# A fused linear-attention and gated feed-forward kernel: five hand-written emission orders replaced

## Chip, cores and metric

The kernel runs on one core of one Trainium2 chip. The metric is the device time of one execution in microseconds. Three executions of the kernel before gave 298.26, 298.84 and 298.95 us; the median, 298.84 us, is the time before.

## What is computed

The inputs are q, k and v of shape 8 x 8 x 576 x 64 (batch, heads, sequence, head size) and three weights: gate and value of 512 x 1536, output of 1536 x 512. First a linear attention, then a gated feed-forward block on its result:

```python
q_s = softmax(q, axis=-1)                      # over the 64 of a head
k_s = softmax(k, axis=2)                       # over the sequence
kv  = einsum('bhsd,bhse->bhde', k_s, v)
x   = einsum('bhsd,bhde->bhse', q_s, kv)       # then 4608 tokens x 512
g   = x @ w_gate
out = (g * sigmoid(g) * (x @ w_val)) @ w_out   # 4608 x 512, float32
```

## The kernel before

**Stages.** The 4608 tokens are worked through in chunks. Batch 0 of the attention is done in a prologue that the change leaves as it is. After it stand nine chunks, each with its own order of work: chunk -1 (tokens 0 to 575, order `PLAN_B`), chunk 0 (tokens 576 to 1023, `PLAN_0`), chunks 1 to 5 (512 tokens each, `PLAN`), chunks 6 and 7 (`PLAN_N`) and chunk 8 (`PLAN_E`), which holds only the rest of the output product. Beside the feed-forward work of its own tokens, chunk ci of 0 to 5 prepares the attention of batch ci+2.

**Orders.** An order is a string of short words, and the kernel emits the instructions of a word when it comes to it. The engines run on their own, but each of them executes its part of the program in the order of emission, and this holds for the DMA queue of SyncE (SP in the profile) too. So a word that is moved is moved in every queue that it has instructions in. A star at a word moves one part of it to another engine.

**Words of the first stage** (`PLAN_B`). `I0` to `I11` multiply 128 columns of the gate weight by the 576 tokens in two PSUM banks; ScalarE (ACT) writes the Silu of them (L321). `J0` to `J11` do it with the value weight, and VectorE (DVE) multiplies by the Silu into `hr` (L326). `Oj1` and `Oj2` are the two halves of the output product of 128 tokens (L479); the second one ends with a copy to `o_sb` and two stores on SP (L468). `Q0` to `Q3` build sums of weight blocks into `gt` (L340). `eq`, `ek` are the exponentials of q and k on ACT (L127), `cv` the cast of v on GpSimd (POOL, L118), `ns` the sum and reciprocal on DVE (L143, L147), `nd` and `nm` the multiplication by it (L152, `nm` on POOL and followed by a DMA transpose on SP, L180). `tr`, `kk` and `xz` finish the attention of batch 1 by TensorE (PE) transposes, and `load:2` issues one load of v.

**Words of the chunks.** The two feed-forward products use a block scheme with seven instead of eight block products (it is Winograd's form of Strassen's). A pair i has the steps `ai`, `bi`, `ci`, `di`, `ei`, `fi`, `gi`, each four matmuls of 256 columns, and `vi`:

- `a`, `c` and `d` copy their PSUM result to a tile `s` by ACT (L116), or by DVE (L118) with a star.
- `v` adds `s` to the bank of `b` on DVE (L412) and takes the Silu on ACT (L414).
- `e` adds on DVE (L422), then multiplies into `hr` on POOL (L423), or on DVE with a star. `f` adds on DVE (L427).
- `g` has a Silu on ACT (L431) and a multiplication into `hr` on POOL (L432), or on DVE with a star. `d`, `f` and `g` accumulate in the bank of `a`, `e` in that of `c`.

`G` and `U` are a plain gate and value product (L441). `A` to `F` and `H` are the seven block products of the output, each twelve matmuls; `B`, `E` and `F` add into `o_sb` on DVE (L553), and `E` and `H` end with four stores each on SP. `Sikn` are sums of `hr` on DVE, `X` and `Y` sums of the attention result (DVE, or POOL with a star), `W` sums of the output weight, `T` a late part of the weight sums. `kv` and `xx` are the two attention products of the next batch; `xx` reads the two transposed tiles `qtd` of that batch, first the one of `nm0`, then that of `nm1`. `pe` and `silu` let ACT load the table of exponentials and of Silu ahead of use. `load` issues the six loads of a later batch on SP.

**Buffers.** PSUM is one pool of eight banks. The Silu results share four buffers (tag `sg`), each kind of `s` tile has two, `o_sb` five.

The instructions that SP gets from `nm`, `E` and `H` come from these lines:

```python
elif nm == "nm":
    norm_mul(b, G, nc.vector if alt else nc.gpsimd)
    tr_dma(b, G)                     # nc.sync.dma_start_transpose
...
elif step == "E":
    self.prod(self.w, self.sum_h(3), self.raw_w(1, 1), False)
    self.add(0, 1, self.w, self.s2)
    self.store(0)                    # four nc.sync.dma_start
```

Of the kernel before, what the change touches and what calls it, by code (L numbers as in the profile page):

```python
# [16 lines left out]
def kernel(  # L17
# [21 lines left out]
    B, H, S, D = q.shape  # L39
# [82 lines left out]
    A, Z = BANKS = ((0, 5), (5, 9))  # L122
# [479 lines left out]
    with tc.manual_schedule():  # L602
# [157 lines left out]
        ORDER = (0, 1, 2, 3, 4, 5)  # L760
        gt2 = [None] * 4
        PLAN_B = """
        I0 I1 pe:1 I2 I3 J0 J1 I4 I5 J2 J3 J4 Q0 I6 J5 I7 J6 J7 eq0:1 ns0:1 eq1:1 I8
        nd0:1* ns1:1 J8 I9 J9 I10 Q1* nd1:1* I11 cv0:1 tr00 J10 J11 tr10 ek0:1 O01 Q3*
        cv1:1 ek1:1 O11 tr01 kk0:1 O02 tr11 eq0:2 O12 kk1:1 ns0:2 O21 xz10* ek0:2 xz00*
        O22 Q2 xz01 eq1:2 cv0:2 xz11 O31 load:2 nm0:2 cv1:2 O32 ek1:2
"""
        PLAN_0 = """
        a0 ns1 G5 b0 G11 Y0 c0 Y2 Y1 v0 Y3* d0* W2 a1 f0 b1 U5 c1 g0 d1 W0 v1 e0 a2 f1 b2
        v2 kv silu:2 nm1 g1 d2 a3 e1 c2 f2 b3 c3 e2 g2 d3 v3 e3 a4 f3 xx* load g3 W1 d4*  # L770
        b4 c4* X0 f4 v4 U11 e4* X2* X1 W3 X3 g4*
"""
        PLAN = """
        a0 S042 b0 G5 c0 d0 A v0 S002 a1 f0 b1 S142 c1 v1 U5 S242 g0 pe S222 B S022 S102
        S122 S302 d1 S322 ek0 e0 a2 S342 e1 eq0 ns0 S202 C ek1 f1 D E eq1 cv1 b2 c2* silu
        F nm0 cv0 g1 d2 v2 ns1 a3 nm1 H* f2 kv g2 d3 b3 c3 v3 e2 load f3 e3 a4 b4 c4 g3 v4
        d4* e4 xx* f4 X2 G11 g4 X0 X1 X3* U11
"""
        PLAN_N = """
        a0 S222 b0 c0 d0 T0* A v0 S002 f0 a1 e0* S042 b1 g0 d1 c1 S022 v1 a2 f1 S242 S102  # L780
        b2 e1* c2 g1 S142 d2 v2 B f2 a3 T1* b3 c3 S342 S122 S202 g2* e2 d3 C S302 v3 f3
        e3* S322 a4 b4 g3* d4 c4 v4 D T2 f4 e4* a5 b5 g4* c5* X0* d5 F f5 v5 E T3* X1 e5*
        X3 g5* H* X2*
"""
        PLAN_E = """
        S022 A S042 S122 S002 S142 S202 B C S102 S302 S322 S242 S222 S342 D E F H*
"""
        chunk(-1, 0, S, PLAN_B)
        chunk(0, S, 1024 - S, PLAN_0)
# [33 lines left out]
```

The softmax here doesn't subtract the row's maximum and nothing guards it: scores larger than these inputs give would overflow.

## Time and profile before

| | |
|---|---|
| median of three runs | 298.84 us |
| the profiled execution | 299.05 us |
| its span, first to last instruction | 297.2 us |
| PE busy | 285.4 us, 96% of the span |
| DVE / ACT / POOL busy | 240.9 / 221.6 / 157.3 us |
| granted TensorE clock | 0.995 of full speed |
| read from / written to HBM | 37.75 / 9.44 MB |

The profiled execution has 1.85 us outside its span and is 0.21 us above the median. Times in the text are counted from the start of the span. The prologue ends at 15.6, chunk -1 at 56.7, chunk 0 at 77.7; the five chunks under `PLAN` take 29.97 us each and end at 227.6, the rest takes what remains. In a row of the timeline the columns are the start, the duration, engine and line, the operation with its tiles, the number of instructions merged into the row, and in brackets the idle time ahead of it and what ended it.

### The profile page before, as it was taken

What the parts mean: (1) busy time and instruction counts of PE and PEld (TensorE: products, weight loads), DVE (VectorE), ACT (ScalarE), POOL (GpSimd) and SP (SyncE); (2) the same over time, 40 slices, a digit from 0 to 9 for tenths busy, and PEclk for the clock granted to TensorE, in tenths of its full rate; (3) what the DMA queues carried; (4) which work ended last, traced back from release to release, by engine and by line L of the source; (5) the groups of instructions that cost most, each with busy time, mean ns of one, the idle gap of its engine ahead of it and who ended that gap; (6) DMA issues with size and microseconds to landing.
All of it is one profiled execution on the core that took longest, in us unless ns stands there. A gap on an engine that the chain in (4) does not pass through costs nothing.

```text
span 297.2 us, 7118 instructions
## 1 busy us (share of the span) xinstructions
PE 285.4 (96%) x2716; PEld 233.2 (78%) x2716; DVE 240.9 (81%) x490; ACT 221.6 (75%) x416; POOL 157.3 (53%) x128
## 2 busy tenths in 40 slices
PE   8999798998999999999999999999999999999992
PEld 6778664587888868886888688868887888888882
DVE  3934696797899888988899789988999898897881
ACT  5784865777799689968896889688969775778431
POOL 1903767679319761976197619771877444031000
PEclk9999999999999999999999999999999999999997
DMA  7999999837902794089517861795092000510065
GB/s 258 293 191 245 242 295 391 263 78 115 391 14 50 151 330 173 20 174 321 189 36 150 268 250 28 151 316 208 21 148 58 0 2 1 108 35 2 8 137 141
DMA packets 38337, 46.46 MB, mean 156 GB/s; under 512 B 16288, under 2 KB 21408, under 8 KB 38304
## 3 DMA queue, kind: packets, MB, share of 16 engines
q1 hardware_dynamic: 32864, 41.03, 48.1%
q0 software_dynamic: 5280, 4.72, 10.1%
q8 instruction: 21, 0.34, 0.5%
q10 hardware_dynamic: 160, 0.26, 0.2%
q14 instruction: 12, 0.10, 0.1%
HBM read 37.75 MB, written 9.44 MB: 159 GB/s over the span
## 4 chain that ended last, share of the span: by engine, by line
PE 72%; DMA 1%; ACT 0%; ACTq 0%; DVE 0%; issue 0%; DVEq 0%
PE sx L388 23%; PE ox L533 13%; PE sw L388 11%; PE ow L533 7%; PE sy L388 6%; PE oy L533 4%; PE u_ps L441 3%; PE g_ps L441 3%; PE kv L192 2%; PE xa L273 1%; DMA out_dram<-o_sb 1%; PE xz L273 0%; ACT o_sb L116 0%; ACTq L468 0%; DVE o_sb L553 0%
## 5 line engine op out<-in xcount | busy, mean ns | idle before, releaser
L388 PEld LDWEIGHTS <-gt 128*128 128x128 f16 x672 | 64.6, 98 | 13.4 <-issue 3.0
L432 POOL TENSOR_TENSOR hr<-sg,u 128x512 bf16<-128x512 f16 (+1 forms) x33 | 39.1, 1184 | 51.8 <-ACT sg L431 50.8
L388 PE MATMUL sx<-xs,gt 128*128 128x256 f16 (+1 forms) x336 | 49.9, 271 | 0.3 <-DVE s L118 0.3
L116 ACT COPY s<-sx 128x512 f32<-128x512 f32 (+1 forms) x77 | 44.3, 577 | 7.7 <-PE sx L388 7.4
L423 POOL TENSOR_TENSOR hr<-sg,u 128x512 bf16<-128x512 f16 (+1 forms) x31 | 36.5, 1184 | 23.1 <-DVE u L422 22.3
L533 PEld LDWEIGHTS <-hs 128*128 128x128 bf16 x384 | 37.3, 98 | 4.6
L152 POOL TENSOR_TENSOR qs<-eq,rr 128x1152 bf16<-128x1152 bf16 x15 | 33.2, 2219 | 9.1 <-DVE rr L147 5.9
L388 PEld LDWEIGHTS <-wg 128*128 128x128 f16 x336 | 32.8, 98 | 4.8
L427 DVE TENSOR_TENSOR u<-sx,s 128x512 f16<-128x512 f32 (+1 forms) x42 | 28.5, 680 | 9.8 <-ACT sg L414 4.0
L414 ACT ACTIVATE sg<-s 128x512 f16<-128x512 f32 (+1 forms) x42 | 26.3, 625 | 12.8 <-DVE s L412 11.0
L431 ACT ACTIVATE sg<-sx 128x512 f16<-128x512 f32 (+1 forms) x42 | 25.2, 600 | 10.7 <-PE sx L388 10.6
L412 DVE TENSOR_TENSOR s<-sy,s 128x512 f32<-128x512 f32 (+1 forms) x42 | 28.4, 677 | 2.9 <-PE sy L388 2.0
L533 PEld LDWEIGHTS <-hr 128*128 128x128 bf16 x288 | 28.1, 98 | 3.3
L422 DVE TENSOR_TENSOR u<-sw,s 128x512 f16<-128x512 f32 (+1 forms) x42 | 28.4, 677 | 2.5 <-PE sw L388 1.2
L143 DVE TENSOR_REDUCE rs<-eq 128x18 f32<-128x1152 bf16 x16 | 21.5, 1342 | 7.0 <-ACT eq L127 7.0
L388 PE MATMUL sx<-xt,gt 128*128 128x256 f16 (+1 forms) x168 | 25.0, 271 | 0.0
L388 PE MATMUL sw<-xs,wv 128*128 128x256 f16 (+1 forms) x168 | 24.9, 271 | 0.0
L388 PE MATMUL sx<-xt,wg 128*128 128x256 f16 (+1 forms) x168 | 24.9, 271 | 0.0
L388 PE MATMUL sy<-xt,wg 128*128 128x256 f16 (+1 forms) x168 | 24.9, 271 | 0.0
L388 PE MATMUL sw<-xs,gt 128*128 128x256 f16 (+1 forms) x168 | 24.9, 271 | 0.0
L116 ACT COPY s<-sw 128x512 f32<-128x512 f32 (+1 forms) x34 | 19.8, 582 | 5.4 <-PE sw L388 5.3
L533 PE MATMUL ox<-wt,hs 128*128 128x256 f16 x192 | 23.6, 273 | 0.0
(101 smaller groups left out, 551.7 us busy)
## 6 DMA issues: line engine op xcount, KB each, us to landing
q<-in_q_dram SPq DMA_DIRECT2D x16, 576.0 KB, 6.9
k<-in_k_dram SPq DMA_DIRECT2D x16, 576.0 KB, 6.5
v<-in_v_dram SPq DMA_DIRECT2D x16, 576.0 KB, 7.5
out_dram<-o_sb SPq DMA_DIRECT2D x70, 128.0 KB, 2.4
wv<-in_moe_w_val_dram POOLq DMA_DIRECT2D x3, 512.0 KB, 11.4
wo<-in_moe_w_out_dram POOLq DMA_DIRECT2D x3, 512.0 KB, 10.7
wg<-in_moe_w_gate_dram POOLq DMA_DIRECT2D x2, 512.0 KB, 11.4
wg<-in_moe_w_gate_dram POOLq DMA_DIRECT2D x2, 256.0 KB, 5.3
```

The source lines that it names most:

```text
L116: nc.scalar.copy(out=out, in_=in_)
L143: nc.vector.reduce_sum(out=rs, in_=s["eq"].rearrange("p t h d -> p (t h) d"), axis=mybir.AxisListType.X)
L152: eng.tensor_mul(s["qs"].rearrange("p t (h d) -> p (t h) d", d=64), s["eq"].rearrange("p t h d -> p (t h) d"), s["rr"].to_broadcast([128, ...
L388: nc.tensor.matmul(out=bank[:, h * j:h * j + h], lhsT=wgt(kk, j), rhs=rhs[:, kk, 0:h], start=first and j == 0 and kk == 0, stop=kk == 1, s ...
L412: nc.vector.tensor_add(self.s1, self.y[:, 0:w], self.s1)
L414: nc.scalar.activation(out=self.sa[:, 0:w], in_=self.s1, func=AF.Silu)
L422: nc.vector.tensor_add(u, self.w[:, 0:w], self.s2)
L423: meng.tensor_mul(self.out(0), self.halves(self.sa), self.halves(u))
L427: nc.vector.tensor_add(self.u, self.x[:, 0:w], self.s5)
L431: nc.scalar.activation(out=sb[:, 0:w], in_=self.x[:, 0:w], func=AF.Silu)
L432: meng.tensor_mul(self.out(1), self.halves(sb), self.halves(self.u))
L533: nc.tensor.matmul(out=dst[p][:, 0:HN], lhsT=lhs(kk, p), rhs=rhs(kk), start=start and i == 0, stop=i == HM - 1, skip_group_check=True,)
```

## The change

All five orders are written anew. Loads, tiles, buffers and every function stay as they are. In `PLAN_B` the first eight `I` and `J` steps stand in groups of four, the words `Q0` and `Q2` move from POOL to DVE and `Q1` from DVE to POOL, `nd0` from POOL to DVE, and the transposes, output products and attention products are placed in another order. `PLAN_0`, `PLAN`, `PLAN_N` and `PLAN_E` hold the same words as before in another order and partly with stars at other words.

```diff
         PLAN_B = """
-        I0 I1 pe:1 I2 I3 J0 J1 I4 I5 J2 J3 J4 Q0 I6 J5 I7 J6 J7 eq0:1 ns0:1 eq1:1 I8
-        nd0:1* ns1:1 J8 I9 J9 I10 Q1* nd1:1* I11 cv0:1 tr00 J10 J11 tr10 ek0:1 O01 Q3*
-        cv1:1 ek1:1 O11 tr01 kk0:1 O02 tr11 eq0:2 O12 kk1:1 ns0:2 O21 xz10* ek0:2 xz00*
-        O22 Q2 xz01 eq1:2 cv0:2 xz11 O31 load:2 nm0:2 cv1:2 O32 ek1:2
+        I0 I1 I2 I3 J0 J1 J2 J3 I4 I5 I6 I7 J4 J5 J6 pe:1 Q2* eq0:1 I8 I9 I10 Q0* ns0:1 J7
+        J8 eq1:1 I11 ns1:1 Q1 nd1:1* J9 J10 O01 cv0:1 ek0:1 J11 O11 O02 nd0:1 tr10 ek1:1
+        tr00 tr01 Q3* O21 kk0:1 cv1:1 O12 eq0:2 tr11 xz01 load:2 kk1:1 ns0:2 nm0:2 cv0:2
+        O31 xz10* xz11* cv1:2 ek0:2 eq1:2 xz00 O22 ek1:2 O32*
 """
         PLAN_0 = """
-        a0 ns1 G5 b0 G11 Y0 c0 Y2 Y1 v0 Y3* d0* W2 a1 f0 b1 U5 c1 g0 d1 W0 v1 e0 a2 f1 b2
-        v2 kv silu:2 nm1 g1 d2 a3 e1 c2 f2 b3 c3 e2 g2 d3 v3 e3 a4 f3 xx* load g3 W1 d4*
-        b4 c4* X0 f4 v4 U11 e4* X2* X1 W3 X3 g4*
+        Y0 a0 b0 Y2 G5 c0 Y1 G11 ns1 d0* Y3* v0 U5 a1 f0 b1 W0 e0 g0* nm1 c1 d1 v1 a2 e1
+        f1 silu:2 b2 v2 kv g1 d2 c2 a3 f2 b3 v3 e2 c3* g2 d3* W1 xx* f3 e3* a4 b4 W2 g3 d4
+        c4 v4 f4 X0 U11 load e4* g4* X2 X1* W3 X3
 """
         PLAN = """
-        a0 S042 b0 G5 c0 d0 A v0 S002 a1 f0 b1 S142 c1 v1 U5 S242 g0 pe S222 B S022 S102
-        S122 S302 d1 S322 ek0 e0 a2 S342 e1 eq0 ns0 S202 C ek1 f1 D E eq1 cv1 b2 c2* silu
-        F nm0 cv0 g1 d2 v2 ns1 a3 nm1 H* f2 kv g2 d3 b3 c3 v3 e2 load f3 e3 a4 b4 c4 g3 v4
-        d4* e4 xx* f4 X2 G11 g4 X0 X1 X3* U11
+        a0 b0 G5 d0 c0 v0 S002 A S042 f0 a1 S022 S142 b1 S222 c1 S102 g0 S122 v1 e0 d1* B
+        S302 pe S322 D S202 f1 S242 S342 eq0 e1 C a2* ek0 ek1 cv1 eq1 ns0 silu nm0 E F cv0
+        b2 ns1 g1 d2 c2 H* v2 a3 f2 nm1 kv g2 b3 d3 c3 v3 e2 a4 load f3 e3 U5 g3 d4* xx b4
+        c4 v4 G11 f4 X0* e4* X2* U11 X1 g4* X3
 """
         PLAN_N = """
-        a0 S222 b0 c0 d0 T0* A v0 S002 f0 a1 e0* S042 b1 g0 d1 c1 S022 v1 a2 f1 S242 S102
-        b2 e1* c2 g1 S142 d2 v2 B f2 a3 T1* b3 c3 S342 S122 S202 g2* e2 d3 C S302 v3 f3
-        e3* S322 a4 b4 g3* d4 c4 v4 D T2 f4 e4* a5 b5 g4* c5* X0* d5 F f5 v5 E T3* X1 e5*
-        X3 g5* H* X2*
+        S002 S202 S022 a0 b0 S222 A d0 c0 v0 a1 f0 S042 b1 S142 e0 c1 g0 d1 v1 B f1 S242
+        S122 S102 a2 C g1 T0 b2 d2 c2 v2 e1 f2 a3 e2* b3 g2 T1* d3 S302 v3 T2* c3* a4 f3
+        b4 D g3 v4 d4* e3* c4 f4 F S342 T3* a5 g4 S322 e4 d5 b5 c5 v5 f5 E X0* X1* e5* g5*
+        X2 H* X3
 """
         PLAN_E = """
-        S022 A S042 S122 S002 S142 S202 B C S102 S302 S322 S242 S222 S342 D E F H*
+        S222 S042 S002 S102 A S242 S022 B S302 S122 S142 S322 C S342 S202 D E F H*
 """
```

## The prediction

> **What bounds the kernel now.** The list of engines on the page comes first, then PE's own waits. In a row of waits stand who waited for whom, the total in us, how often, and the longest.
>
> ```profile
> PE 285.4 (96%) x2716; PEld 233.2 (78%) x2716; DVE 240.9 (81%) x490; ACT 221.6 (75%) x416; POOL 157.3 (53%) x128
> ```
>
> ```profile
> PE g_ps L310 <- ACT sg L321: 1.5, 1, 1.5
> PE kv L192 <- POOL vb L118: 1.4, 1, 1.4
> PE xa L273 <- DVE wt L492: 1.3, 1, 1.3
> ...
> PE sx L388 <- DVE s L118: 0.3, 1, 0.3
> ```
>
> PE bounds it, and an order can win only where PE waits. The timeline of PE places the waits; the two of chunk -1 end here:
>
> ```profile
> 37.07 2.26 PE L310 MATMUL g_ps<-xt,wg 128*128 128x320 f16 x16 [1.54 <-ACT sg L321]
> ...
> 46.37 0.70 PE L192 MATMUL kv<-vb,ek 64*128 64x129 bf16 x18 [1.40 <-POOL vb L118]
> ```
>
> The other two begin at 60.3 and 72.3 (chunk 0): 4.5 us together. From 77.7 to the last matmul PE never waits; four matmuls take 0.437 us, twelve 1.31, a plain product 0.87, `kv` 1.16. So the early orders can win **at most 4.5 us**, and the seven later chunks can only lose.
>
> The wait at 72.3 is put down to DVE, but the weight queue names the real one, the transposed tile `qtd`:
>
> ```profile
> PEld L273 <- DMA qtd<-qs: 1.6, 1, 1.6
> ```
>
> So `xx`, which reads both `qtd` tiles, is the place where a queue of SP can stop PE. SP's own timeline, chunk 3 of the kernel before:
>
> ```profile
> 153.66 2.43 SPq L468 DMA_DIRECT2D out_dram<-o_sb  x4
> 156.19 4.75 SPq L180 DMA_TRANSPOSE qtd<-qs  x2
> 161.04 3.40 SPq L468 DMA_DIRECT2D out_dram<-o_sb  x4
> ```
>
> The reader is to see the order: four stores of `E`, both transposes, four stores of `H`. The second transpose is issued at 159.7, 0.07 us after POOL ended `nm1`, and `xx` begins at 164.2. Twelve transposes landed 3.2 us after issue in nine cases, and after 4.5 to 5.0 in three.
>
> **What the Trainium skill says.** "DMA: Bandwidth & Descriptors", section "Anatomy of one DMA": a semaphore wait happens on the issuing sequencer before dispatch. So what stands behind a waiting DMA on SP waits too; the trace agrees, with the two transposes as one stretch of 4.75 us in which the stores behind them, whose data was ready at 157.6, were not issued. "SBUF — State Buffer", section "SBUF: two separate sides": DVE with two SBUF inputs and POOL exclude each other for a whole instruction; a sum of 0.41 us lasts 1.36 at 139.2, beside POOL's sum of 139.16 to 140.31. "ScalarE: Activation LUTs", section "What ACT_TABLE_LOAD costs": about 1283 ns; the trace has 1.28.
>
> **PLAN_B, part by part.** Landing times are those of before: value weights at 18.7, 23.8 and 31.6, gate weights by 26.4, q of batch 1 at 31.2 and 34.1, v at 44.7 and 47.5, k at 42.1 and 46.1.
> - *`I` and `J` in groups of four.* 24 steps of 0.98 us from 15.64, each weight landed before its step. At `pe` the order drops no table load (six before and after). `I8` to `I10` get their Silu at 33.8 to 35.8 behind `eq0` (31.3 to 32.5) and a load of 1.28, so `J8` waits for a bank about 0.2. Then ACT has `eq1`, a load on each side, and `I11`: 35.8 + 1.28 + 1.16 + 1.28 + 0.71 = 40.2. PE comes to `J11` at 39.8: 0.2. The old wait of 1.54 was this chain with nothing to cover it; now `J9`, `J10` and `O01` (3.3 us) do.
> - *`Q0`, `Q2` to DVE, `Q1` to POOL.* DVE does four sums of 1280 columns at 0.82 from 31.7, POOL being idle, instead of POOL at 2.6 each; `Q1` takes POOL from 35.1 to 40.3, `nd1` to 42.4, before v lands. DVE pays with `J7` to `J9`, done 3 us late; banks of `I8` to `I10` cover it. If not, each later `J` costs up to 0.8.
> - *`O` words ahead of the attention.* `O01`, `O11`, `O02` need the output weights (35.5, 38.0, 40.6) and fill the time to 44.1; `O21` fills to 46.4, when `cv0` has ended at about 46.2. The 1.40 goes.
> - *`load:2` ahead of four stores and `nm0`.* v is issued at about 52 instead of 55.9 and lands near 57; `cv1:2` ends at 58.2, before `Y3` and `kv`.
>
> Sum: 2.94 of waits go, 0.4 come; with 0.5 of smaller shifts either way chunk -1 ends 2.5 earlier.
>
> **PLAN_0.** `nm1` moves up: `e0`'s product ends on POOL at 62.9, `nm1` at 65.0, its transpose lands at 68.3, and `xx` stands at 68.1 with its first half of 0.3 us: the 1.3 goes, so does the 0.33. New waits come from DVE's and ACT's longer queues (W0, W1, stars at `c3`, `d3`): `g0` behind `f0`'s addition 0.4, `f3` behind `d3`'s copy 0.35, `f4` behind `d4`'s copy (ACT does all of `xx*` first) 0.35. Gain 0.5. **Both early chunks: 3.0**; from both sides, 4.5 if no new wait comes and 1.0 if each is twice as long and the transpose lands in 5.0.
>
> **PLAN, five chunks.** DVE gains `d1*`, `a2*` for `c2*` (0), `e4*`, `g4*` (0.7), the odd parts of `xx` (1.3), and loses one X sum (0.4): +1.6 us on 26.4 busy of 29.97. Walking the queues with 0.60 between DVE additions, each PE step keeps at least 0.4 us to the addition or copy that it waits for; if that cover goes, the excess is lost per chunk.
>
> The moved DMAs are the cost. `nm0` now comes ahead of `E`, and `nm1` behind `H`: SP has **transpose, four stores, four stores, transpose**, and the six loads right behind. Both sides are counted from the end of `a2` on PE:
> - To the second half of `xx`: `E`, `F`, `H` 3 x 1.31, sixteen pair steps x 0.437, `kv` 1.16 and 0.1 of change-over, `U5` 0.87, the first half of `xx` 0.3 = **13.35**.
> - To the second `qtd`: handoff 0.1, `a2`'s copy on DVE 0.6, `ns0` 1.64 (reduce 1.34, reciprocal), handoff 0.13, `nm0` 2.2 (2.12 to 2.30), handoff 0.07, transpose 1.31, eight stores at 0.61 with 0.3 of gaps 5.2, transpose to landing 3.2 = **14.45**.
>
> PE waits **1.1 us** in `xx` in each of five chunks: 5.5 in all. `nm1` itself ends some 2 us before its turn and hides. What is late behind: the copies of `xx`, `X0` and the next `a0`, all shifted alike. The bounds: 0.6 with the shorter `nm0` and a store pitch of 0.59; 2.9 with a landing of 5.0; store groups of 3.40 and 4.05 us are seen too.
>
> **PLAN_N and PLAN_E.** With `C` early, its banks are held to `E`, and four remain for pairs; `c2` begins some 0.15 after `g1`'s Silu: 0 to 0.3 for two chunks. In `PLAN_E` DVE adds for `B` before `S142`, so `D` (3.93 after `A`) waits to 4.1: 0.2. The tail behind `H` is the same. Together +0.3.
>
> **The sum.** -3.0 + 5.5 + 0.3 = +2.8 on the profiled execution (299.05, of which 297.2 is span and 1.85 around it). That stands 0.21 above the median of three, within which the estimate can't be told apart; on the median, 298.84 + 2.8 = 301.6, of which I take **301.5**.
>
> **The rivals.**
> - *Faster: the transpose is in time.* If SP issues stores and transpose 1.1 us sooner than the rows say (`nm0` earlier, stores back to back at the 0.47 seen for single ones), PE finds `qtd` landed, and the early gain stays: 298.84 - 3.0 + 0.3 = 296.1, down to 294.6. For it speak the 4 us that the new order leaves between `nm1`'s end and `xx` (4.6 before); against it that all ten groups of four stores took 2.4 us or more. It decides where the SP chain loses 1.1 of 14.45; at 0.5 us of wait per chunk the two effects cancel.
> - *Much slower: the transpose lands late.* The transpose at 68.5 had the six loads issued right behind it, as all of them now would, and took 5.0. Four chunks with loads behind at 1.8 more, and chunk 0's `xx` at 1.3: 301.5 + 8.5 = 310. Against it: 4.5 was also seen at 216.1 with no loads behind, so loads may not be the cause.
> - *No change:* the early gain and the waits cancel, at 298.8. So it would also look if chunk -1 gained and `PLAN` never met its transpose by small shifts.
>
> **How the numbers follow.** About 0.3% (0.9 us) is what a measurement of this kernel tells from no change. The base case has 0.50, with its own range 299.8 to 304; the late transpose 0.18; the transpose in time 0.22; no change 0.10. So faster 0.22, same 0.10, slower 0.68. The range from 295.5 to 307 leaves out the best of the fast case and most of the late one.
>
> **What would show it.** Right: chunk -1 ends near 54.2, chunk 0 near 74.7, no wait of over 0.5 at L310 and `kv`; then a wait at L273 for DMA `qtd` in each of chunks 1 to 5, near 1.1 us, with a period of 31.1, and SP's rows in the order named. Wrong: a period of 29.97 in those chunks, or a wait that DVE ends in them; or waits of the old size at 35 and 45.

## The result and the profile after

| | before | after |
|---|---|---|
| median of four runs | 298.85 us | **311.14 us** (310.26 to 312.8) |
| the profiled execution | 299.05 us | 310.26 us |
| its span | 297.2 us | 308.3 us |
| granted TensorE clock | 0.995 | 0.988 |

The kernel became slower: time after by time before is **1.042**, with an interval of 1.038 to 1.047. That is +12.3 us where +2.7 was forecast, and outside the range given. The profiled execution is the fastest of the four, so 1.1 of the 12.3 us have no trace. Of the runs of the experiments further down, two (317.32 us of `only_PLAN` and 301.15 of `nm1_ahead_of_H`) lie over 1.5% above the fastest of their kernel and are left out of the medians and ratios.

**By stages.** The first matmul of each chunk splits the 11.1 us between the two spans (it starts up to 0.15 before the last one of the chunk ahead has ended, so chunk 0 ends at 77.59 here):

| stage | before | after | difference | forecast |
|---|---|---|---|---|
| chunk -1 ends at | 56.70 | 53.78 | -2.92 | -2.5 |
| chunk 0 takes | 20.89 | 22.04 | +1.15 | -0.5 |
| the five chunks of `PLAN` take | 149.83 | 163.08 | **+13.25** | +5.5 |
| the rest takes | 69.78 | 69.40 | -0.38 | +0.3 |

So the question is where 13.25 us in `PLAN` come from. The page's list of engines, busy us and share of the span, comes first. PE does the same 2716 instructions in 3.9 us more busy time, and DVE and ACT work less than before:

```profile
PE 289.3 (94%) x2716; PEld 234.6 (76%) x2716; DVE 238.6 (77%) x515; ACT 211.6 (69%) x391; POOL 150.0 (49%) x128
```

PE's waits in the kernel after (who waited for whom: total us, times, longest):

```profile
PE xa L273 <- DMA qtd<-qs: 9.3, 5, 2.7
PE sw L388 <- POOL xs L354: 1.3, 1, 1.3
...
PE sx L388 <- ACT s L116: 0.9, 3, 0.4
PE kv L192 <- POOL vb L118: 0.7, 1, 0.7
```

The two large waits of chunk -1 at L310 and `kv` have shrunk to one of 0.7. In their place stand five waits in `xx` for the transposed tile `qtd`, one in each `PLAN` chunk. In PE's timeline their ends are at these rows, with the idle time in brackets:

```profile
102.84 0.33 PE L273 MATMUL xa<-qtd,kn 64*64 64x320 bf16 x4 [1.23 <-DMA qtd<-qs]
...
134.45 0.33 PE L273 MATMUL xa<-qtd,kn 64*64 64x320 bf16 x4 [1.53 <-DMA qtd<-qs]
...
167.21 0.33 PE L273 MATMUL xa<-qtd,kn 64*64 64x320 bf16 x4 [2.67 <-DMA qtd<-qs]
...
201.48 0.33 PE L273 MATMUL xa<-qtd,kn 64*64 64x320 bf16 x4 [2.50 <-DMA qtd<-qs]
...
234.60 0.33 PE L273 MATMUL xa<-qtd,kn 64*64 64x320 bf16 x4 [1.37 <-DMA qtd<-qs]
```

They add up to 9.30 us. Three are near the forecast 1.1; two are more than twice that. SP's timeline shows the order that was expected, here in chunk 3:

```profile
155.86 1.26 SPq L180 DMA_TRANSPOSE qtd<-qs  x1
157.22 5.07 SPq L468 DMA_DIRECT2D out_dram<-o_sb  x8
162.39 1.33 SPq L180 DMA_TRANSPOSE qtd<-qs  x1
163.77 0.60 SPq L89 DMA_DIRECT2D q<-in_q_dram  x1
```

Transpose, eight stores, transpose, loads; before, it was four stores, two transposes, four stores. The second transpose was issued at 162.39 and landed 4.8 us later, when `xx` could go on.

The waits leave about 4 us of the 13.25 unexplained. The timeline of PE right behind the wait of chunk 3 has them:

```profile
168.03 1.06 PE L388 MATMUL sw<-xs,gt 128*128 128x256 f16 x4
168.88 1.91 PE L441 MATMUL g_ps<-xt,wg 128*128 128x512 f16 x4
170.59 1.02 PE L388 MATMUL sx<-xs,gt 128*128 128x256 f16 x4
171.44 0.60 PE L388 MATMUL sw<-xs,wv 128*128 128x256 f16 x4
```

Four matmuls of 256 columns last 1.06 instead of 0.60, and the row of 512 columns 1.91 instead of 1.03. The table by windows gives the granted clock (the column behind POOL's busy time) in steps of 1.5 us around this wait:

```profile
165.00:166.50 1.50, 0.00 (x0) 0.00 (x0) 0.41 (x2) 0.00 (x0) 0.82 (x1) 1.00 0.32 48
166.50:168.00 1.50, 0.79 (x12) 0.53 (x13) 0.38 (x2) 0.42 (x3) 0.00 (x0) 1.00 1.06 369
168.00:169.50 1.50, 1.50 (x8) 0.90 (x7) 1.37 (x3) 0.94 (x3) 0.18 (x1) 0.51 1.06 393
169.50:171.00 1.50, 1.50 (x6) 0.59 (x4) 0.00 (x0) 0.85 (x3) 0.97 (x1) 0.50 1.06 393
171.00:172.50 1.50, 1.50 (x11) 0.98 (x9) 0.76 (x2) 0.48 (x1) 0.75 (x1) 0.86 1.06 393
```

PE is idle, starts again, and then has **half its clock for 3.4 us** (168.03 to 171.44). In that time it does 1.7 us of work, so 1.7 us are lost. The same happens behind the wait that ends at 201.48, from 202.4 to 205.7; behind the three short waits the clock stays at 1.00. The four runs of this kernel had mean clocks of 0.979 to 0.989. So the five chunks are +9.3 of waits, +3.4 of clock and 0.55 of smaller shifts.

### The profile page after: what moved, and what is told of

The parts are those of the page before. It is cut to its first block, busy times and chain, and to the rows that moved or that the text cites. A ratio compares the mean times of both kernels' runs of the same rounds, so it can differ in the third digit from the quotient of the medians.

```text
span 308.3 us, 7123 instructions
## 1 busy us (share of the span) xinstructions
PE 289.3 (94%) x2716; PEld 234.6 (76%) x2716; DVE 238.6 (77%) x515; ACT 211.6 (69%) x391; POOL 150.0 (49%) x128
## 4 chain that ended last, share of the span: by engine, by line
PE 73%; DMA 15%; DVE 3%; ACT 2%; SPq 2%; issue 1%; POOL 1%; ACTq 0%; DVEq 0%; POOLq 0%
PE sx L388 20%; PE ox L533 13%; PE sw L388 11%; PE ow L533 7%; DMA qtd<-qs 6%; PE sy L388 6%; DMA v<-in_v_dram 5%; PE g_ps L310 4%; PE oy L533 3%; PE g_ps L441 3%; PE u_ps L310 2%; PE kv L192 2%; DMA q<-in_q_dram 2%; PE u_ps L441 2%; DMA k<-in_k_dram 2%
## 5 line engine op out<-in xcount | busy, mean ns | idle before, releaser
L388 PEld LDWEIGHTS <-gt 128*128 128x128 f16 x672 | 65.7, 99 | 15.3 <-issue 2.8
L432 POOL TENSOR_TENSOR hr<-sg,u 128x512 bf16<-128x512 f16 (+1 forms) x33 | 38.7, 1173 | 50.8 <-ACT sg L431 50.6
L423 POOL TENSOR_TENSOR hr<-sg,u 128x512 bf16<-128x512 f16 (+1 forms) x29 | 33.1, 1143 | 39.1 <-DVE u L422 23.5
L116 ACT COPY s<-sx 128x512 f32<-128x512 f32 (+1 forms) x65 | 37.7, 581 | 10.5 <-PE sx L388 10.1
L152 POOL TENSOR_TENSOR qs<-eq,rr 128x1152 bf16<-128x1152 bf16 x14 | 29.8, 2131 | 10.8 <-DVE rr L147 10.5
L116 ACT COPY s<-sw 128x512 f32<-128x512 f32 (+1 forms) x39 | 22.8, 586 | 4.7 <-PE sw L388 4.4
L388 PE MATMUL sw<-xs,gt 128*128 128x256 f16 (+1 forms) x168 | 25.9, 278 | 0.0
```

The costliest lines, as they stand in the source:

```text
L116: nc.scalar.copy(out=out, in_=in_)
L152: eng.tensor_mul(s["qs"].rearrange("p t (h d) -> p (t h) d", d=64), s["eq"].rearrange("p t h d -> p (t h) d"), s["rr"].to_broadcast([128, ...
L388: nc.tensor.matmul(out=bank[:, h * j:h * j + h], lhsT=wgt(kk, j), rhs=rhs[:, kk, 0:h], start=first and j == 0 and kk == 0, stop=kk == 1, s ...
L423: meng.tensor_mul(self.out(0), self.halves(self.sa), self.halves(u))
L432: meng.tensor_mul(self.out(1), self.halves(sb), self.halves(self.u))
```

## The experiments

Three theories stood against each other. **A:** SP's order in `PLAN` makes the waits, and the longer ones bring a second loss through the clock. **B:** it is something else in `PLAN`, either DVE, whose stars were moved, or the six loads that now stand right behind the transpose and make it land late. **C:** the clock fell for a reason that has nothing to do with the waits. The first four kernels ran on one chip, where the kernel before had a median of 298.37 us in 31 runs; the last three on another, with 298.55 in 21. A ratio is always to the kernel before.

**1. `only_PLAN`: the kernel before with nothing new but `PLAN`.**

> The kernel before with the new PLAN alone (PLAN_B, PLAN_0, PLAN_N, PLAN_E as before). Theory A: the whole loss comes from PLAN: waits in xx of five chunks of 1.2 to 2.7 and the clock behind the long ones, together +11 to +14 us, so 310 to 313. If the loss needs the new early orders as well: below 305.

Measured: 311.62 us, ratio 1.044 (1.039 to 1.048), with five waits in `xx` of chunks 1 to 5 of 1.45, 1.50, 2.47, 2.44 and 1.52 us; the five chunks took 161.8. So this one order carries the whole loss. Here too chunks 3 and 4 have the long waits. The clock fell behind only one of them, as PE's timeline shows at the row of 512 columns:

```profile
168.69 0.33 PE L273 MATMUL xa<-qtd,kn 64*64 64x320 bf16 x4 [2.47 <-DMA qtd<-qs]
...
169.94 1.03 PE L441 MATMUL g_ps<-xt,wg 128*128 128x512 f16 x4
...
201.21 0.33 PE L273 MATMUL xa<-qtd,kn 64*64 64x320 bf16 x4 [2.44 <-DMA qtd<-qs]
...
202.69 1.91 PE L441 MATMUL g_ps<-xt,wg 128*128 128x512 f16 x4
```

**2. `nm1_ahead_of_H`: the kernel after with one word moved.** The transpose of `nm1` is issued ahead of the four stores of `H`; everything else of the five orders stays.

```diff
-        b2 ns1 g1 d2 c2 H* v2 a3 f2 nm1 kv g2 b3 d3 c3 v3 e2 a4 load f3 e3 U5 g3 d4* xx b4
+        b2 ns1 g1 d2 c2 nm1 H* v2 a3 f2 kv g2 b3 d3 c3 v3 e2 a4 load f3 e3 U5 g3 d4* xx b4
```

> The changed kernel with nm1 (POOL product and transpose) emitted just ahead of H* in PLAN, so that SP has transpose, four stores of E, transpose, four stores of H; POOL's order is the same as in the changed kernel. Theory A (the stores of H hold the second transpose on SP, PE waits for it in xx, and the clock falls after the long waits): the transpose is issued some 2.5 us sooner, against waits of 1.2 to 2.7, so no wait is left in chunks 1 to 5 or 0.2 at most, no clock below 1.00 there, a period of 29.97 to 30.2, and 296.5 to 298 us. Rival B (DVE's longer list in PLAN, or landings of 5.0 because of the loads): waits of 1 us or more remain in xx or go over to L388 and L427, and the time stays above 305.

Measured: 297.3 us, ratio 0.997 (0.995 to 0.999); the five chunks took 149.6, no wait in `xx` is left, and the clock is 1.00 in all five. SP's timeline in chunk 2 of this kernel:

```profile
126.53 1.29 SPq L180 DMA_TRANSPOSE qtd<-qs  x1
127.94 2.81 SPq L468 DMA_DIRECT2D out_dram<-o_sb  x4
130.87 1.34 SPq L180 DMA_TRANSPOSE qtd<-qs  x1
132.32 2.44 SPq L468 DMA_DIRECT2D out_dram<-o_sb  x4
```

Four stores between the two transposes instead of eight: the second one follows the first after 4.3 us instead of 6.5 to 7.9, and that is enough for every chunk, also for chunk 4, where it landed after 4.3. With 149.6 against 149.83 nothing else in `PLAN` costs anything; DVE's stars and sums are the same as in the kernel after, so a DVE that is too full would have shown. This half of B falls.

**3. `nm0_behind_E`: the kernel after with the first transpose behind the stores of `E`.** SP has four stores, transpose, four stores, transpose, and the six loads still right behind the second one.

```diff
-        S302 pe S322 D S202 f1 S242 S342 eq0 e1 C a2* ek0 ek1 cv1 eq1 ns0 silu nm0 E F cv0
+        S302 pe S322 D S202 f1 S242 S342 eq0 e1 C a2* ek0 ek1 cv1 eq1 ns0 silu E nm0 F cv0
```

> The changed kernel with nm0 emitted behind E in PLAN instead of ahead of it, so that SP has four stores of E, transpose, four stores of H, transpose, and the six loads right behind the second transpose as in the changed kernel. Theory A: E's stores leave before nm0 is ready, the second transpose goes out about 1.5 to 2 us sooner; the waits of 1.2 to 1.5 go, and 0 to 0.7 is left where a store or the transpose is slow; 297 to 300 us. Rival B (loads right behind a transpose make it land after 5.0): landings near 5.0 in chunks 1 to 4, waits of 1 us or more, above 303.

Measured: 298.64 us, ratio 1.001 (0.998 to 1.004); the five chunks took 151.1. Of PE's waits this view has what is left in `xx`, 0.99 in chunk 2 and 0.26 in chunk 4:

```profile
PE xa L273 <- DMA qtd<-qs: 1.2, 2, 1.0
```

Both stand in chunks in which a group of four stores took longer (3.90 and 3.65 us instead of 2.4). The four second transposes with the six loads behind them landed after 3.2 or 3.3 us, and the one without loads after 3.2. So loads behind a transpose do not make it late, and the other half of B falls. Why does moving the first transpose help the second? The stores of `E` no longer wait behind a transpose that waits for `nm0`: they go while POOL still computes. In chunk 1 they end 0.45 us after `nm0` on POOL, so not all of their 2.4 us is saved: the second transpose is issued 22.1 us behind the chunk's first matmul instead of 23.7.

**4. `fill_10`: the waits filled with work.** Ten matmuls on a zero tile are put between the two halves of `xx` in chunks 1 to 5; their result is not used. If the clock falls because PE is idle, it must now stay up, although `qtd` comes as late as before. (Two lines are added, so line numbers behind them are higher by 2.)

```diff
             s = st.pop((b, G))
+            if G == 1 and 3 <= b < B:
+                warm_up(10)
             for t0, t1 in BANKS:
```

> The changed kernel with ten matmuls of 256 columns on the tile of zeros between the two halves of xx in chunks 1 to 5 (1.07 us of PE time that computes nothing used). PE is busy for the first 1.07 us of each wait. Theory A (clock falls because PE stands idle for more than about 2 us): the waits end at the same time, idle time left is 0.2 to 0.5 in three chunks and 1.5 in the two long ones, the clock stays at 1.00, and the time falls by the 3.4 us of slow clock, to 306.5 to 308. Rival C (the clock falls for another reason than the wait): no gain, 310 to 311.5, clock at 0.50 for some 3.4 us in some chunks as before.

Measured: 309.1 us, ratio 1.034 (1.028 to 1.040), between the two times expected. In the profiled run the five chunks took 158.7 instead of 163.1. The timeline of PE in chunk 3:

```profile
168.30 1.26 PE L256 MATMUL warm_ps<-zero 128*128 128x256 bf16 x10
170.35 0.33 PE L275 MATMUL xa<-qtd,kn 64*64 64x320 bf16 x4 [0.79 <-DMA qtd<-qs]
...
171.17 0.60 PE L390 MATMUL sw<-xs,gt 128*128 128x256 f16 x4
171.61 1.03 PE L443 MATMUL g_ps<-xt,wg 128*128 128x512 f16 x4
172.47 0.60 PE L390 MATMUL sx<-xs,gt 128*128 128x256 f16 x4
172.91 0.60 PE L390 MATMUL sw<-xs,wv 128*128 128x256 f16 x4
```

The wait is now 1.26 of work and 0.79 of idle time, and the same three steps behind it take 1.74 us (171.17 to 172.91) instead of 3.41. The clock is 1.00 in all five chunks. Of the 4.4 us, 3.4 are the two lost stretches; 1.0 is that chunks 3 and 4 met shorter delays on SP in this run. For that reason this run does not show by itself that the filling held the clock: from the end of the first half of `xx` to the start of the second are 1.99 us in chunk 3 and 2.15 in chunk 4, so by this estimate the waits would also without filling have been shorter than any that a drop followed.

What settles it are the traces together. In the nine kernels traced, the recorded clock falls five times between the prologue and the last matmul, and each time right behind a PE wait of 2.44 us or more. In experiments 2 and 3, which take the long waits out of the five chunks, it does not fall there; in chunk 0 of `nm1_ahead_of_H` and `fill_10` it falls behind waits for another engine. So **idle PE lowers its own clock**, and the cost of a long wait is not its length alone.

C falls. In the profiled run of `fill_10`, 309.64, most of that gain is lost again ahead of it: like the profiled run of `nm1_ahead_of_H` it has another wait in chunk 0, of 3.0 us (3.3 there), for POOL at the line of `Y3`, with a clock drop behind it, and chunk 1 begins 3.6 us later than in the kernel after. That led to the second set, on the early orders.

**5. `only_B`: the kernel before with the new `PLAN_B` alone.**

> Before with only the new PLAN_B; the other four orders are the old ones. The early gain is measured by itself. If the 2.92 us that chunk -1 gained in the changed kernel belong to PLAN_B alone, chunk -1 ends near 53.8 (before 56.7). Chunk 0 then tells what the earlier v load costs: v(2,1) is issued at about 52 instead of 55.9. Theory: POOL's cv1:2 waits for that load, and Y3*, which stands behind it on POOL, comes late for PE; in PLAN_0 of before Y3* stands a few words later in front of W2 than in the new one, so the wait should be under 1.0 us here and chunk 0 should keep 2 to 2.9 of the gain: 296.0 to 297.0. Rival (the gain of chunk -1 is only lent, since v's landing sets the start of chunk 0 whatever PLAN_0 says): a wait of 1.2 to 3 us for POOL at L354 or kv in chunk 0, and a time of 297.5 to 299. Five PLAN chunks 149.9 in both.

Measured: 297.15 us, ratio 0.995 (0.992 to 0.997). Chunk -1 ends at 53.95, so its gain belongs to `PLAN_B`. Chunk 0 takes 21.40 instead of 20.89, with the two old waits, now 0.33 and 1.06, and chunk 1 begins 2.24 us earlier than before. The time of 297.15 lies just above the theory's 296.0 to 297.0 and below its rival's 297.5, and there is no wait for `Y3`.

**6. `B_and_0`: the kernel before with the new `PLAN_B` and `PLAN_0`.**

> Before with the new PLAN_B and PLAN_0; PLAN, PLAN_N and PLAN_E are the old ones. It is the part that the forecast put at -3.0. Measured by the stages of the changed kernel it should be -1.9 on the profiled run where the wait for Y3 in chunk 0 is 1.3, so 296.9; with a wait of 3.2 and the clock drop behind it, as two other runs showed, about +1, so 299.8. Theory (Y3 behind cv1:2 on POOL): a wait at L388 for POOL L354 of 1 to 3.3 us stands near 60, no wait over 0.5 in xx of chunks 1 to 5, and those five chunks take 149.9. Rival (the five chunks are slower because of how the new early orders hand over to them, not because of PLAN): five chunks over 152 here.

Measured: 298.43 us, ratio 0.999 (0.997 to 1.002), in twelve runs from 297.67 to 300.08. The part of the change that was forecast at -3.0 is worth nothing that can be measured: `PLAN_0` gives back what `PLAN_B` brings. The wait for `Y3` is there with 1.02, and the five chunks take 150.0, so `PLAN` needs nothing from the early orders to be as fast as before. The profiled run (299.51) is one of the longer ones of the twelve: its chunk -1 ended at 55.80, in part for a wait of 0.37 for ACT's copy to `kn` that `only_B` does not have, so its stages are not those of the median.

**7. `Y3_on_DVE`: `nm1_ahead_of_H`, and one star removed in `PLAN_0`,** so that the sum `Y3` is done by DVE and no longer stands behind the cast `cv1:2` on POOL.

```diff
-        Y0 a0 b0 Y2 G5 c0 Y1 G11 ns1 d0* Y3* v0 U5 a1 f0 b1 W0 e0 g0* nm1 c1 d1 v1 a2 e1
+        Y0 a0 b0 Y2 G5 c0 Y1 G11 ns1 d0* Y3 v0 U5 a1 f0 b1 W0 e0 g0* nm1 c1 d1 v1 a2 e1
```

> The changed kernel with nm1 ahead of H in PLAN and with Y3 on DVE instead of POOL in PLAN_0, so that it no longer stands behind cv1:2. If Y3 behind the cast is what stops PE at 60 in the changed early orders, that wait of 1.1 to 3.3 us is gone, and the clock drop of the longer ones too: chunk 0 ends 1.3 to 3 us earlier than with nm1 ahead of H alone (297.31), so 295.0 to 296.3. A wait at kv for the cast of v may remain, since kv reads the same cast. Rival (v's landing is the bound in itself, and the wait only moves from Y3 to kv): a wait at kv for POOL L118 of over 0.5 us in chunk 0, and 297 to 297.5 again. Rival (DVE is full there): e0 or g0 waits for DVE by 0.4 or more and the gain is under 0.5.

First the timeline of POOL in the kernel after:

```profile
58.19 1.15 POOL L118 CAST vb<-v 128x1152 bf16<-128x1152 f32 x1 [2.99 <-DMA v<-in_v_dram]
59.29 1.03 POOL L354 TENSOR_TENSOR xs<-xt,xs 128x448 f16<-128x448 f16 x1
```

and of its PE, at `e0`:

```profile
60.38 0.54 PE L388 MATMUL sw<-xs,wv 128*128 128x224 f16 x4 [1.27 <-POOL xs L354]
```

POOL idles for 3 us because its next instruction, the cast, waits for v. The sum behind it needs nothing of v, but stands in the same queue, and PE waits for the sum. In `Y3_on_DVE` the timeline of DVE has that sum, and PE's timeline the same step without a wait:

```profile
58.26 0.38 DVE L354 TENSOR_TENSOR xs<-xt,xs 128x448 f16<-128x448 f16 x1
```

```profile
59.20 0.55 PE L388 MATMUL sw<-xs,wv 128*128 128x224 f16 x4
60.29 0.54 PE L388 MATMUL sx<-xt,gt 128*128 128x224 f16 x4 [0.54 <-DVE u L427]
```

Measured: **296.15 us, ratio 0.991 (0.989 to 0.993)**, the best of all kernels tried, in six runs from 295.86 to 296.63. Chunk 0 takes 20.90 and the five chunks 149.45. The same kernel without this edit, experiment 2, had a ratio of 0.997 (0.995 to 0.999) on the other chip. The theory holds: v landed no earlier than in the kernel after (6.4 us after its issue, against 6.2), and no wait moved to chunk 0's `kv`. The rival of a full DVE has a small part in it: the step behind, `g0`, now waits 0.54 for `f0`'s addition.

## Why the prediction was wrong in its size

**What held.** PE bounds the kernel, an early order could win only its 4.5 us of waits, and the later chunks could only lose. The new wait was named with its place (the second half of `xx`), its cause (the transposed tile behind eight stores on SP) and its count (five). Of the waits named for chunk 0, `f4` at 0.35 came with 0.29; `f3` did not wait, but `f2` and `d4` did, by 0.38 and 0.27, for ACT's copies of `d2` and `a4`, which were not named; and `g0` at 0.4 shows with 0.54 once the larger wait ahead of it is gone. The old wait in chunk 0's `xx` went, as worked out. Chunk -1 won 2.92 for 2.5.

**Where the miss lies.** In spans it is 8.3 us, 11.1 for 2.8: 3.8 too little for the waits in `xx`, 3.4 for the clock, which was put at nothing, 0.55 for smaller shifts in `PLAN`, and 1.65 for chunk 0; chunk -1 and the last stages give back 0.4 and 0.7.

**Step "PE waits 1.1 us in `xx` in each of five chunks: 5.5 in all".** Its working was good, its use of it was not. In chunk 1 the first transpose was issued 4.81 us after the end of `a2` (4.74 by the sum of the rows), the second 6.71 after that (6.51), it landed after 3.2, and PE waited 1.23. The three ordinary chunks have 1.23, 1.53 and 1.37. But in two of five something on the way to the transpose's landing took over a microsecond longer, and the wait is 2.67 and 2.50. The DMA view of the kernel after, from 191 to 199 us in 40 slices of 0.2 us, shows how in chunk 4:

```profile
GB/s 0 0 91 223 216 207 209 212 196 244 143 174 174 308 225 184 318 164 184 256 215 164 31 10 10 10 10 20 20 246 195 174 195 236 215 164 215 195 215 215
...
q8 instruction: 1, 0.02, 1.2%
```

For 1.4 us (195.4 to 196.8) almost nothing moves, in the midst of the stores, and one packet of an instruction queue (an instruction fetch) falls in this window, at 194.0 to 194.6; the eight stores then took 6.38 us instead of 5.2. In chunk 3 a like gap (165.0 to 166.2) lies in the landing of the transpose. `only_PLAN` has its long waits in the same two chunks. The kernel before has such gaps too: they are in the group of 4.05 us in its chunk 2 and of 3.40 in its chunk 3. There the transposes had slack, and PE saw nothing of them. The prediction saw those two groups, and three of twelve landings at 4.5 to 5.0, and used them for its bounds only. **Once a chain has no slack, each of its delays is paid in full**, and so the sum has to take means, not usual values. The ten groups of stores in the kernel before have a mean of 2.70 us, so eight stores come to 5.5 with the gap between, 0.3 more than the 5.2 used; the twelve landings have a mean of 3.6, 0.4 more than 3.2. That makes 1.8 us per chunk instead of 1.1, and 1.86 was measured. The miss is 9.3 for 5.5, 3.8 us, of which 3.0 come from the two chunks. This sum was made afterwards, with the result known. Whether the fetch causes the gap is open. In the two chunks it stands 0.4 to 1.4 us ahead of the gap, but a fetch at 138 to 140, in the midst of loads, has no gap behind it, and no kernel was made to test it. The lower bound of 0.6 does not follow from the two terms named for it either, which bring 1.1 down to some 0.85.

**A term that was missing: the clock.** +3.4 us. The Trainium skill, "TensorE: Matmul & The Clock Gate", section "What's actually happening", says that TensorE runs at half clock after an idle window of about 3.4 us and needs a busy one of the same length to come back, and that the windows run freely. The length agrees with this trace: 3.4 us at 0.50. The trigger doesn't quite, and here the measurement decides: waits of 2.50 and 2.67 us were enough, as were 3.0 and 3.3 in chunk 0 of two other kernels; near 2.45 one dropped and one did not; of the waits up to 1.53 none did.

A table by windows in steps of 0.05 us places the changes. The two slow stretches begin at 168.02 and 202.15 and last 3.41 us each; their beginnings are 34.13 apart, ten times 3.413, and the drop behind the last matmul, at 307.97, is 31 times 3.413 later. In `only_PLAN`, `nm1_ahead_of_H` and `fill_10` the slow stretch and the drop behind the last matmul are 31, 68 and 71 such steps apart. So the clock changed only on a grid of 3.413 us, as windows that run freely would make it. The cases fit if what counts is how long PE stood idle within one step: it was 2.40 to 2.99 us in the step ahead of each of the five drops. The wait of 2.47 that no drop followed lies across two steps, with 1.87 in the one and 0.60 in the other.

A wait that is estimated at 1.1 is safe from it and one of 2.5 is not, so the clock belonged into the upper bound of the range: 2.9 of wait can cost 4.6.

**Step "v is issued at about 52 instead of 55.9 and lands near 57; `cv1:2` ends at 58.2, before `Y3` and `kv`".** The load was issued at 51.85, but landed 6.2 us later instead of some 5: it was issued 2.5 us after four stores of 128 KB had begun, at over 300 GB/s of traffic, where before the traffic had already sunk to 72 to 82 GB/s. The cast ended at 59.3, `Y3` at 60.3, and `e0` waited 1.27. The new order had a load, a cast and a sum in one chain with no slack. That is the larger part of why chunk 0 is at +1.15 for -0.5: with `Y3` on DVE it takes 20.90 us instead of 22.04. The waits listed for chunk 0 are 2.2 us against 1.6 before; the rest is spread over gaps too small to be listed. Over many runs the early gain that was put at -3.0 came to -0.1 us by the medians (`B_and_0`), less than the profiled run has. With `Y3` on DVE the gain is at 2.7 by the start of chunk 1.

**DVE, "+1.6 us on 26.4 busy" in each chunk of `PLAN`.** Over the five chunks DVE was busy 131.1 us, where 133.65 stood before. The sums of `hr` at L502 and L506, which lasted 0.72 and 0.64 us in the mean, lasted 0.41; what shortened them was not tested. No wait hung on it.

**`PLAN_N` and `PLAN_E`, "Together +0.3".** Measured -0.4, with 0.1 in `PLAN_N` and nothing in `PLAN_E`; the tail is 0.4 shorter. No wait of the kind named (`c2`, `D`) is in the list.

**The rivals.** The late transpose gave 310 and so nearly the right time, by luck and for the wrong reason: it put four landings at 5.0 because of the loads behind, and a wait of 1.3 in chunk 0. One of the four landed after 4.8, the others after 3.2 or 3.3, chunk 0's `xx` did not wait, and experiment 3 has the loads behind without late landings. What was to decide for the fast rival, SP earlier by 1.1, is what experiment 2 did on purpose.

## What to carry to other kernels

Where two transfers with a fixed queue between them end just in front of their reader, count the slack in each repetition, and charge it with every delay that the trace of before shows on that queue, also those that cost nothing there. Price an idle TensorE by its wait and, where the wait can fill some 2.4 us of one step of the clock's grid, by another 1.7 us. When a load is issued earlier, look at which in-order queue holds the instruction that waits for it, and move what does not need the load out of that queue.

## What the runs showed of the hardware

- Five of six TensorE waits of 2.44 to 3.25 us were followed by 3.41 us at a granted clock of 0.50, in which 1.7 us of work were lost; waits of up to 1.53 us never were. The clock changed only on a grid of 3.413 us; PE had been idle for 2.40 us or more of the step ahead of each of these five drops, and for 1.87 where the sixth wait had none.
- All traffic of the DMA engines fell to 6 to 19 GB/s for 0.8 to 1.4 us in two chunks each of the kernels before and after, in the midst of stores or of a transpose's landing.
- A DMA transpose took SP 1.3 us to issue and landed after 3.2 us in the median, with six loads right behind it or none.
- The load of v of batch 2, issued at 51.7 to 53.9 us behind four stores, landed after 5.9 to 7.5 us in seven kernels; issued at 55.7 to 55.9, in the two with the old `PLAN_B`, it landed after 4.8.
